# The first segment's attention by halves of its queries, each half through all heads, with the output projection to follow each half

## The chip, the cores and the metric

The kernel runs on one core of a Trainium2 chip. The metric is the device time of one launch in microseconds (us). A run has a *granted clock*: the mean share of TensorE's full clock that the chip allowed in that run.

Engine names are those of the profile: PE is TensorE (matmul), PEld its weight load, DVE is VectorE, ACT is ScalarE, POOL is GpSimd, SP is the queue that issues most transfers. L1205 is line 1205 of the kernel; the changed kernel has other line numbers for the same things.

## The reference, cut to what matters

T = 2048 tokens of D = 640, H = 32 heads of 20, four segments of L = 512, and a feed-forward width of 1728. Attention is causal inside a segment; a memory M carries over from segment to segment.

```python
def layer(x):
    x = x + attention(layernorm(x))     # wq, wk, wv, wo, memory
    x = x + relu(layernorm(x) @ w1) @ w2
    return x

def attention(xn):                       # for each head
    for s in range(4):
        p = softmax(q[s] @ k[s].T * scale + causal_mask)
        o = g * (phi(q[s]) @ M) / (phi(q[s]) @ z) + (1 - g) * (p @ v[s])
        outs.append(o)
        M = M + phi(k[s]).T @ v[s]; z = z + phi(k[s]).sum()
    return concat(outs) @ wo

out = layer(layer(x))                    # same weights in both layers
```

The first segment of the first layer has no memory yet. Nothing of its output projection, its second layer norm or its feed-forward can start before its attention is done, and at that point of the program there is little else to do but the projections of queries, keys and values.

## The kernel before

The kernel does not write its instruction order down. It describes each piece of work as a small generator, with the engines that may run it, a modelled duration, and what it needs and holds; a list scheduler inside the kernel builds the order on each engine. It makes 20 plans, and keeps the one that its own model says ends first. So any edit of a duration or a dependency may reorder the whole program. The parts that matter:

```python
HALVES = (0,)      # in segment 0 the scores go out four matmuls at a time, X and Y apart
...
# PSUM: X and Y (2 banks each) for scores, OD (1 bank) for p @ v, MISC (3 banks) for all else

def scores(m):                 # a pair of head groups (4 heads each), all 512 queries
    rounds = (((0, 0, 0),), ((0, 1, 0), (0, 3, 384)), ((0, 2, 0), (1, 2, 256)),
              ((1, 0, 0),), ((1, 1, 0), (1, 3, 384)))        # 5 rounds, each 512 columns wide
    ...
    def make(parts, ks):       # matmuls with K = 20: four heads in four row groups of the array
        ... e.matmul(ps[:, hh, o:o + N], kq(b, gg[x], 0)[32*hh:32*hh + DH, 128*j:128*j + 128],
                     kq(b, gg[x], 1)[32*hh:32*hh + DH, 128*j:L])
    def exp(u, k, bs, tk): ... # ACT: 1024 elements per partition into the tile PT
    def mask(x, j, ex): ...    # POOL: affine_select on the diagonal blocks of PT

def apply(n): ...              # p @ v: 128 x 32 matmuls in four column groups, into OD
def o_turn(a, s): ...          # waits for all heads, transposes o, then the output projection
```

One setup step is also touched by the change. `kqL` holds the query and key rows of the last heads, and it is cleared once, on POOL, before it is written:

```python
def consts():
    ...
    tl = yield pool(1600.0, lambda e: e.memset(kqL[:], 0.0))
    KQL[0].drop(tl)                                  # writers of kqL wait for it
    tm = yield pool(400.0, lambda e: e.memset(maskg[:], 0.0))
```

The softmax here doesn't subtract the row's maximum and nothing guards it: scores larger than these inputs give would overflow.

## Time and profile before

The time before was 592.19 us, the median of 3 runs (592.14 to 592.25). The page of the kernel before, its first two parts, begins like this; the second part gives the busy tenths in 40 equal slices:

```profile
span 591.0 us, 12433 instructions
...
PE 575.2 (97%) x5086; PEld 297.3 (50%) x5086; DVE 425.9 (72%) x1018; ACT 427.3 (72%) x520; POOL 215.5 (36%) x342
...
PE   8989999999999899999999999999999999999998
...
ACT  4869999989888888878787776897787787123140
...
PEclk9979999999999999999999999999999999999999
```

TensorE is called busy for 97% of the span. That busy time contains what happens inside pipelined matmuls, so I also computed a *useful share*: the columns streamed in a stretch, divided by 2.4 GHz and by the length of the stretch. 2.4 GHz is the clock that the prediction takes; the traces come close to it, as two whole matmuls of 512 columns start 0.216 us apart. Matmuls in row groups or column groups run four at a time (16 of `p @ v`, 5,120 columns in all, take 0.73 us) and are counted as a quarter. A matmul that runs over the edge of a stretch is counted in both, so the shares are about 0.01 too high. For 40 to 60 us the groups by shape of the kernel before begin with these (line, names, shapes, count, then busy time and mean):

```profile
L912 PE MATMUL ps<-wv_r,xnT 128*128 128x320 bf16 x21 | 5.2, 301 | 0.0
L878 PE MATMUL ps<-xnT,wk_p 128*128 128x512 bf16 x13 | 4.3, 385 | 0.0
L1011 PE MATMUL ps<-wb,hT 128*128 128x512 bf16 x10 | 3.3, 423 | 0.0
L878 PE MATMUL ps<-xnT,wq_p 128*128 128x512 bf16 x10 | 2.7, 380 | 0.0
...
```

These four rows stream 21 x 320 + 33 x 512 = 23,616 columns, or 9.8 us at 2.4 GHz. The scores add 2.1 us and the `p @ v` matmuls 2.1 us. So 14.0 of 20 us are streaming: a useful share of 0.70, where the page says 100% busy.

| Stretch (us) | 0–20 | 20–40 | 40–60 | 60–80 | 80–100 | 100–120 | 120–140 | 140–160 |
|---|---|---|---|---|---|---|---|---|
| useful share before | 0.52 | 0.58 | 0.70 | 0.75 | 0.87 | 0.78 | 0.83 | 0.90 |

One place stands out in the first 40 us. The timeline of the kernel before (start, duration, engine, line, operation, what it waited for) shows a POOL memset, two DVE items that last as long as it does, and TensorE waiting for one of them:

```profile
29.89 2.92 DVE L989 COPY hT<-ident 128x48 bf16<-128x48 bf16 x3
30.14 2.65 POOL L741 MEMSET kqL<- 128x3072 bf16 x1
30.23 2.76 DVE L826 TENSOR_SCALAR xn_tok<-x_sb,mv,rstd 128x640 bf16<-128x640 bf16 x1
33.04 0.45 PE L790 MATMUL ps<-ident,xn_tok 128*128 128x128 bf16 x5 [1.82 <-DVE xn_tok L826]
```

Just after it, the busy time by stretches (the number after POOL's is the granted clock) shows TensorE at half clock:

```profile
34.00:36.00 2.00, 2.00 (x22) 0.59 (x20) 1.28 (x3) 0.90 (x1) 0.96 (x2) 0.58 0.78 189
36.00:38.00 2.00, 2.00 (x16) 0.58 (x9) 1.61 (x9) 1.15 (x2) 0.08 (x1) 0.50 0.60 228
38.00:40.00 2.00, 2.00 (x6) 0.56 (x4) 0.18 (x2) 0.68 (x2) 1.22 (x2) 0.50 0.73 131
40.00:42.00 2.00, 2.00 (x14) 0.67 (x14) 0.41 (x1) 1.63 (x3) 0.00 (x0) 0.71 1.05 200
```

Finally, the chain of waits of the kernel before, between 46 and 68 us (start, duration, what), is almost only exponentials on ACT:

```profile
47.04 3.75 ACT PT L1219 x4
50.79 1.83 ACT PT L1216 x2
52.62 3.67 ACT PT L1219 x4
...
62.73 3.67 ACT PT L1219 x4
```

### The profile page before, as it was taken

To read this page: it belongs to the slowest core of one execution; us is meant where nothing else is said; L and a number is where in the kernel's file an instruction comes from. 1 tells how busy PE (TensorE), PEld (TensorE's weight loads), DVE (VectorE), ACT (ScalarE), POOL (GpSimd) and SP (SyncE) were. 2 spreads that over 40 slices of the span, in tenths; PEclk is the share of its full clock that TensorE was granted. 3 is DMA by queue.
4 is the path that set the end of the run, shared out by engine and by line. 5 is a ranking of instruction groups with operands and counts; after the bars stand their busy time and mean duration, and the time that the engine had idled before them with its cause. 6 is when DMAs were issued, how large, how long until landed. Compare 5 with 4: busy or idle time off the path is not lost.

```text
span 591.0 us, 12433 instructions
## 1 busy us (share of the span) xinstructions
PE 575.2 (97%) x5086; PEld 297.3 (50%) x5086; DVE 425.9 (72%) x1018; ACT 427.3 (72%) x520; POOL 215.5 (36%) x342
## 2 busy tenths in 40 slices
PE   8989999999999899999999999999999999999998
PEld 4423345434565354564444555455544654655655
DVE  6769769999979974899755985597827898734202
ACT  4869999989888888878787776897787787123140
POOL 4556644745343543344433440344322333002000
PEclk9979999999999999999999999999999999999999
DMA  6244593494743531256329314254408451331201
GB/s 211 91 110 102 101 166 66 57 216 95 106 84 70 110 64 37 41 109 118 63 32 150 52 26 88 43 94 89 68 2 105 101 92 31 84 69 23 68 0 45
DMA packets 126609, 48.44 MB, mean 82 GB/s; under 512 B 114056, under 2 KB 125256, under 8 KB 126552
## 3 DMA queue, kind: packets, MB, share of 16 engines
q1 hardware_dynamic: 124600, 40.10, 38.2%
q0 software_dynamic: 1520, 7.21, 4.0%
q8 instruction: 40, 0.66, 0.4%
q10 hardware_dynamic: 432, 0.34, 0.2%
q14 instruction: 17, 0.14, 0.1%
HBM read 13.77 MB, written 6.06 MB: 34 GB/s over the span
## 4 chain that ended last, share of the span: by engine, by line
PE 76%; DVE 13%; ACT 6%; DMA 3%; issue 1%; POOL 0%; SPq 0%
PE ps L1486 20%; PE ps L1466 16%; PE ps L878 13%; PE ps L1418 7%; PE ps L1205 7%; PE ps L1287 6%; PE ps L912 5%; ACT PT L1219 4%; DMA wb<-in_A_wk_dram 2%; DVE hT L1449 1%; ACT PT L1216 1%; DVE xn_tok L826 1%; DVE o_sb L1336 1%; PE ps L1155 1%; DMA oT<-o_sb 1%; DVE o_sb L1144 1%
## 5 line engine op out<-in xcount | busy, mean ns | idle before, releaser
L1219 ACT ACTIVATE PT<-ps 128x1024 bf16<-128x1024 f32 x256 | 248.3, 1031 | 49.9 <-PE ps L1205 49.1
L1195 POOL TENSOR_SCALAR_AFFINE_SELECT PT<-PT 128x512 bf16<-128x512 bf16 x256 | 172.2, 689 | 266.3 <-ACT PT L1219 220.1
L1466 PE MATMUL ps<-xnT,wb 128*128 128x512 bf16 x560 | 135.4, 380 | 3.0 <-DVE hT L1449 3.0
L1486 PE MATMUL ps<-wb,hT 128*128 128x320 bf16 x896 | 131.9, 299 | 0.6 <-DVE o_sb L1144 0.5
L1360 DVE TENSOR_TENSOR x_sb<-x_sb,ps 128x320 bf16<-128x320 bf16 x128 | 60.9, 479 | 69.8 <-PE ps L1486 53.4
L1486 PEld LDWEIGHTS ps<-wb,hT 128*128 128x128 bf16 x896 | 83.5, 98 | 39.6 <-issue 7.8
L1466 PEld LDWEIGHTS ps<-xnT,wb 128*128 128x128 bf16 x560 | 50.5, 98 | 63.5 <-issue 7.6
L1450 ACT ACTIVATE hT<-ps 128x512 bf16<-128x512 f32 x54 | 32.3, 598 | 56.8 <-PE ps L1466 56.5
L1216 ACT ACTIVATE PT<-ps 128x1024 bf16<-128x1024 f32 x64 | 62.2, 1028 | 10.9 <-PE ps L1205 10.7
L912 PE MATMUL ps<-wv_r,xnT 128*128 128x320 bf16 x320 | 60.3, 300 | 1.5 <-DVE va L900 0.6
L865 DVE CAST kq<-ps 128x512 bf16<-128x512 f32 x44 | 30.1, 686 | 36.4 <-PE ps L878 36.4
L878 PE MATMUL ps<-xnT,wk_p 128*128 128x512 bf16 x200 | 55.3, 381 | 0.0
L878 PE MATMUL ps<-xnT,wq_p 128*128 128x512 bf16 x200 | 54.8, 386 | 0.1
L1418 PE MATMUL ps<-wo_r,oT 128*128 128x320 bf16 x320 | 52.6, 300 | 1.2 <-DMA oT<-o_sb 0.9
L1449 DVE TENSOR_SCALAR hT<-ps 128x512 bf16<-128x512 f32 x58 | 39.4, 681 | 8.2 <-PE ps L1466 7.7
L912 PEld LDWEIGHTS ps<-wv_r,xnT 128*128 128x128 bf16 x320 | 29.6, 98 | 23.0 <-issue 3.9
L1287 PE MATMUL ps<-PT,va 128*32 128x128 bf16 (+3 forms) x896 | 40.7, 302 | 0.0
L826 DVE TENSOR_SCALAR xn_tok<-x_sb,mv,rstd 128x640 bf16<-128x640 bf16 x64 | 37.0, 590 | 4.8 <-DMA xnT<-xn_tok 3.6
L1418 PEld LDWEIGHTS ps<-wo_r,oT 128*128 128x128 bf16 x320 | 29.7, 98 | 18.6 <-issue 3.8
L1205 PE MATMUL ps<-kq 20*128 20x512 bf16 (+3 forms) x560 | 35.3, 301 | 0.1
L813 DVE BATCH_NORM_STATS2 stats<-x_sb 128x6 f32<-128x320 bf16 x64 | 29.7, 465 | 2.8 <-DMA x_sb<-in_A_x_dram 2.5
L1287 PEld LDWEIGHTS ps<-PT,va 128*32 128x32 bf16 x896 | 18.9, 96 | 23.7 <-issue 11.2
(100 smaller groups left out, 617.7 us busy)
## 6 DMA issues: line engine op xcount, KB each, us to landing
kq_scr<-kq SPq DMA_DIRECT2D x28, 120.0 KB
kqL<-kq_scr SPq DMA_DIRECT2D x28, 120.0 KB
out_dram<-x_sb SPq DMA_DIRECT2D x16, 160.0 KB, 1.8
wb<-in_B_w_dram POOLq DMA_DIRECT2D x5, 432.0 KB, 3.5
x_sb<-in_A_x_dram POOLq DMA_DIRECT2D x3, 640.0 KB, 5.5
wb<-in_B_w_dram POOLq DMA_DIRECT2D x2, 640.0 KB, 6.9
xnT<-xn_tok SPq DMA_TRANSPOSE x52, 2.7
wv_r<-in_A_wv_dram SPq DMA_DIRECT2D x1, 800.0 KB, 7.2
```

Of the source, the lines that this page charges most:

```text
L878: fn = lambda e, bank, k=k, w_p=w_p, c=c: e.matmul(bank, w_p[:, k, c * 128:(c + 1) * 128], xnT[:, k_, :, k, :], start=(k == 0), stop=(k == ...
L912: fn = lambda e, bank, k=k, i=i, hf=hf: e.matmul(bank[:, 0:320], xnT[:, k_, i, k, :], wv_r[:, k, hf * 320:(hf + 1) * 320], start=(k == 0), ...
L1195: tm = yield pool(590.0, lambda e: e.affine_select(out=reg, in_=reg, pattern=[[0, 4], [1, 128]], compare_op=ALU.is_ge, fill=0.0, base=0, c ...
L1205: fns.append((lambda e, x=x, j=j, hh=hh, N=N, o=o: e.matmul(ps[:, hh, o:o + N], kq(b, gg[x], 0)[32 * hh:32 * hh + DH, 128 * j:128 * j + 12 ...
L1216: fn = lambda e: e.activation(PT[:, :, 2 * k:2 * k + 2, 1024:1280], bs.ap.rearrange("p h (x t) -> p x h t", x=2), ACT.Exp, scale=SCALE)
L1219: fn = lambda e: e.activation(PT[:, items[0], 2 * k:2 * k + 2, c0:c0 + 512], bs.ap, ACT.Exp, scale=SCALE)
L1287: return [(lambda e, hh=hh, j=j: e.matmul(bank[32 * hh:32 * hh + 32, 128 * j:L], v_flat[b][:, (j * H + 8 * hh + g) * E1:(j * H + 8 * hh + ...
L1360: ta = yield dve(320, 1, lambda e: e.tensor_tensor(xa, xa, bk.ap[:, 0:320], ALU.add), [tk], early=HOT)
L1418: fn = lambda e, bank, k=k, hf=hf, o=ot.ap: e.matmul(bank[:, 0:320], o[:, k, :], wo_r[:, k, hf * 320:(hf + 1) * 320], start=(k == 0), stop ...
L1449: th = yield evac(512, 1, lambda e: e.tensor_scalar(hTv[:, dc, :], bk.ap, 0.0, None, ALU.max), lambda e: e.activation(hTv[:, dc, :], bk.ap ...
L1466: fn = lambda e, bank, k=k, dc=dc: e.matmul(bank, w1_r[:, k, dc * 128:(dc + 1) * 128], xnT[:, k_, :, k, :], start=(k == 0), stop=(k == FC ...
L1486: fn = lambda e, bank, dc=dc, i=i, hf=hf: e.matmul(bank[:, 0:320], hTv[:, dc, i * 128:(i + 1) * 128], w2_r[:, dc, hf * 320:(hf + 1) * 320] ...
```

## The change

The intent: take the queries of the first segment in two halves. The first half (256 queries) goes through all heads, then the second. The output projection of the first half can then start while the second half is in attention, and TensorE gets other work earlier. The rounds become 512 and 256 wide in the first half, and 512, 384, 512, 384 in the second. The output of each half is turned by TensorE transposes instead of DMA transposes. Two small things came along: the memset of `kqL` is dropped (it is not needed for the result), and the scheduler is told that weights land 1.7 us later. Core of the diff, cuts marked:

```diff
-        HALVES = (0,)
+        HALVES = tuple((m, v) for m in range(4) for v in range(2))
+        FFN_HALVES = ()
+        FIRST_ORDER = ((0, 0), (1, 0), (0, 1), (2, 0), (3, 0), (1, 1), (2, 1), (3, 1))
...
-            def ld(e, name, nbytes, fn, key, waits=(), issue=700.0, lat=2600.0):
+            def ld(e, name, nbytes, fn, key, waits=(), issue=700.0, lat=4300.0):
...
-            KQL[0].take()
...
-                tl = yield pool(1600.0, lambda e: e.memset(kqL[:], 0.0))
-                KQL[0].drop(tl)
...
-            def scores(m):
+            def layout(m, hv):      # hv: None for whole, 0 or 1 for a half
+                ...
+                if hv == 0:
+                    at = {(x, j): (m % 2, (256 * x, 512 + 128 * x)[j], 128 * j, 256 - 128 * j)
+                          for x in range(2) for j in range(2)}
+                    return at, (((0, 0), (1, 0)), ((0, 1), (1, 1)))
+                at = {(x, j): (x, 256 * j, max(256, 128 * j), 128 if j == 3 else 256) ...}
+                return at, (((0, 0), (0, 1)), ((0, 2), (0, 3)), ((1, 0), (1, 1)), ((1, 2), (1, 3)))
+            def scores(m, hv):
...
+            def turn_half(m, hv, g, od, tk):
+                ...
+                    return [(lambda e, i=i: e.transpose(
+                        bf(bank)[:, i * 128:(i + 1) * 128], rw.ap[:, 0, i * 128:(i + 1) * 128], ident[:]),
+                        i == NJ - 1) for i in range(NJ)]
+                ...
+                S.set("oh", hv, m, v=to)
...
                 for i in range(NJ):
+                    if a * NSEG + s == 0 and i % 2 == 0:      # o_turn: wait for this half only
+                        ow = []
+                        for m in range(G // 2):
+                            r = yield Need("oh", i // 2, m)
+                            ow += r
```

The feed-forward also learns to run by halves (`FFN_HALVES`), but that list is left empty.

## The prediction

> **What bounds the kernel now.** The page gives TensorE 97% busy, but that counts waits inside pipelined matmuls. I divided the columns streamed in each stretch (groups by shape) by the 2.4 GHz of the Trainium skill, "TensorE: Matmul & The Clock Gate" (score and apply matmuls four at a time). The useful work is then about 58% of the time in 20–40 us, 70% in 40–60, 75% in 60–80, 78–87% in 80–140, and 0.86–0.93 afterwards. So TensorE bounds the kernel from about 80 us on, and the recoverable loss is early: against 0.89, some 15 us between 20 and 130 us. There the exponentials on ACT set the pace (chain of waits: 47–67 us is almost only ACT PT; ACT busy 0.9–1.0 of 40–120), because nothing of output projection or feed-forward can start until the first segment's attention is finished: exponentials of segment one end at 66 us, first output projection matmul at 94.5 us, first W1 matmul at 115.7 us.
>
> A second loss, beside it: the timeline shows the POOL memset of kqL taking 2.65 us at 30.1–32.8, and in just that time small DVE copies (L989) and one normalisation (L826) take 2.9 and 2.8 us instead of about 0.1 and 0.45. "SBUF — State Buffer", section "Who interferes with whom", states that a GpSimd instruction and a 2-port DVE instruction exclude each other; the trace agrees. TensorE waits 1.82 us there for xn_tok, and the granted clock is 0.5 from about 34.3 to 41 us (windows of 1 us): about 3 us more.
>
> **What the change does.** It removes that memset and builds the selectors of the relay at the very start, where DVE is idle. It adds 8 exponentials (48 in place of 40 in the first segment, same elements; fixed part of one about 0.1 us: 1 us on ACT), 32 transposes of 128x128 on TensorE (0.09 us each: 3 us, in slack), and takes away 4 DMA transposes with their latency. The narrower exponentials (about 0.5 and 0.7 us instead of 0.94) leave less time to refill the other PSUM pair: an estimated 2 us of ACT idle. The first exponential comes about 0.8 us later (both heads' groups needed).
>
> What it moves: by instruction order, when the first segment's exponentials are all issued, TensorE has done 11 us more useful work than before (49.6 against 38.7), 12 us more after the second segment's; still 9 at half of the attention, 5 at three quarters. ACT has 8 us more done at the first of these points.
>
> **On the critical path.** ACT must do about 102 us of work to the end of the second segment's exponentials (97 before). I expect that point at about 121 us (before 120.5) with work done that before had at about 131 us. Later DVE (0.95–1.0 busy in 90–160 us) and ACT, lagging, give back a part. Net gain 5 to 10 us: predicted 584.5 us, range 577.5 to 591. Faster by over 2% 0.20, within 2% 0.77, slower 0.03.
>
> **What would show it.** Useful TensorE share in 20–80 us up from 0.68 to about 0.75–0.8; no 2.7 us DVE copies at 30 us and no half clock in the 30–40 us stretch (TensorE waits under 1 us); first output projection near 75 us or earlier; first W1 matmul at 105–112 us; segment-one exponentials ending at 70–76 us; ACT busy +1 to +2 us in total; stretches after 160 us shifted, not changed.
>
> **What would make it wrong.** A new TensorE gap in the first 40 us with another half-clock spell (slower: gain gone). ACT idling at each narrow round, more than 5 us in total. Orders made for modelled durations, in which in-order waits on DVE give the lead back at 100–160 us. Or the gain lies mostly in the memset: then the halves alone give nothing.

## More of the kernel before

Scores, `p @ v` and all other matmuls use the array in three different groupings: by row groups, by column groups, and whole. The scheduler knows that changing costs something; it reckons 100 ns for each change (`MODE_NS = 100.0`).

## The result, and the profile after

The changed kernel took 591.65 us, the median of 4 runs (590.17 to 592.00), beside 592.22 us for the kernel before on the same chip (4 runs, 592.14 to 593.39). The ratio is 0.9981 with a 95% interval of 0.996 to 1.0002: the same time. A ratio here and below is the mean time of one kernel's fast runs over that of the other's of the same rounds, so it is not quite the ratio of the medians that I quote. The prediction, 584.5 us with a range of 577.5 to 591.0, was missed: the measured median lies above the range.

The page of the changed kernel, its first lines and the granted clock:

```profile
span 590.3 us, 12794 instructions
...
PE 576.7 (98%) x5257; PEld 302.2 (51%) x5257; DVE 424.4 (72%) x1027; ACT 429.7 (73%) x531; POOL 210.2 (36%) x341
...
PEclk9999999999998999999999999999999999999999
```

The stall at 30 us is smaller, and the half clock behind it is gone. But at 187 us a new wait of TensorE appears. The timeline of the changed kernel:

```profile
30.52 1.50 DVE L750 CAST maskg<-gt 20x160 bf16<-20x160 f32 x1
...
33.08 0.45 PE L789 MATMUL ps<-ident,xn_tok 128*128 128x128 bf16 x5 [1.24 <-DVE xn_tok L825]
...
187.15 0.59 PE L1543 MATMUL ps<-xnT,wb 128*128 128x512 bf16 x2 [1.38 <-DMA xnT<-xn_tok]
```

Its busy time by stretches has full clock after the first wait and half clock after the second:

```profile
34.00:36.00 2.00, 2.00 (x16) 1.30 (x14) 1.89 (x8) 1.92 (x5) 0.00 (x0) 1.00 0.41 146
...
186.00:188.00 2.00, 0.78 (x10) 0.24 (x10) 2.00 (x10) 1.76 (x2) 1.52 (x3) 1.00 0.51 132
188.00:190.00 2.00, 2.00 (x26) 0.74 (x19) 2.00 (x5) 1.75 (x2) 1.08 (x2) 0.53 0.66 128
190.00:192.00 2.00, 2.00 (x6) 0.59 (x4) 1.38 (x4) 0.19 (x1) 1.22 (x2) 0.62 0.59 82
```

| | before | after |
|---|---|---|
| last exponential of segment one ends (us) | 66.4 | 76.0 |
| last exponential of segment two ends | 120.5 | 129.9 |
| first output projection matmul | 94.5 | 63.0 |
| first W1 matmul | 113.6 | 107.4 |
| useful share 20–40 us | 0.58 | 0.78 |
| useful share 40–60, 60–80 | 0.70, 0.75 | 0.70, 0.74 |
| useful work done by 40 / 80 / 180 / 260 us | 21.8 / 50.4 / 133.9 / 202.4 | 25.9 / 54.0 / 139.2 / 204.8 |

The lead of 4.1 us of useful work is made before 40 us, where the memset was. It does not grow in 40 to 80 us, where the halves are at work, and it falls to 2.3 us between 180 and 260 us, the stretch that begins with the half clock. Of what is left, about 1.7 us is the 32 added transposes of 128 columns (32 x 128 / 2.4 GHz), which are not useful in the end.

The chain of waits of the changed kernel in the same part of the program is no longer ACT's. It runs through many short pieces of TensorE:

```profile
57.07 0.33 PE ps L1347 x4
57.40 0.32 PE ps L1221 x4
57.72 0.54 PE ps L877 x2
58.48 0.27 PE ps L1221 x4
58.75 0.54 PE ps L877 x2
59.69 0.50 PE ps L1314 x16
60.19 0.32 PE ps L877
```

### The profile page after: what moved, and what is told of

Same layout as the page of the kernel before. It is cut to its first block, busy times and chain, and to the rows that moved or that the text cites. A ratio compares the mean times of both kernels' runs of the same rounds, so it can differ in the third digit from the quotient of the medians.

```text
span 590.3 us, 12794 instructions
## 1 busy us (share of the span) xinstructions
PE 576.7 (98%) x5257; PEld 302.2 (51%) x5257; DVE 424.4 (72%) x1027; ACT 429.7 (73%) x531; POOL 210.2 (36%) x341
## 4 chain that ended last, share of the span: by engine, by line
PE 73%; DVE 18%; ACT 6%; issue 1%; POOL 1%; DVEq 0%
PE ps L1543 17%; PE ps L1565 17%; PE ps L877 13%; PE ps L1221 7%; PE ps L911 6%; PE ps L1314 5%; PE ps L1489 5%; ACT PT L1239 4%; DVE x_sb L1426 2%; DVE hT L1517 2%; ACT etmp L1057 1%; DVE stats L812 1%; DVE stats L813 1%; DVE xn_tok L825 1%; DVE phq L1124 1%
## 5 line engine op out<-in xcount | busy, mean ns | idle before, releaser
L1239 ACT ACTIVATE PT<-ps 128x1024 bf16<-128x1024 f32 (+1 forms) x272 | 256.3, 1000 | 45.0 <-PE ps L1221 43.7
L1209 POOL TENSOR_SCALAR_AFFINE_SELECT PT<-PT 128x512 bf16<-128x512 bf16 x256 | 168.8, 677 | 269.6 <-ACT PT L1239 229.4
L1543 PE MATMUL ps<-xnT,wb 128*128 128x512 bf16 x560 | 137.9, 382 | 2.0 <-DMA xnT<-xn_tok 1.4
L1518 ACT ACTIVATE hT<-ps 128x512 bf16<-128x512 f32 x53 | 31.7, 599 | 52.8 <-PE ps L1543 52.6
L1236 ACT ACTIVATE PT<-ps 128x1024 bf16<-128x1024 f32 x56 | 54.3, 1025 | 14.9 <-PE ps L1221 14.7
L1489 PE MATMUL ps<-wo_r,oT 128*128 128x320 bf16 x320 | 54.0, 300 | 0.9 <-DVE x_sb L1426 0.7
L877 PE MATMUL ps<-xnT,wk_p 128*128 128x512 bf16 x200 | 53.8, 381 | 0.0
L864 DVE CAST kq<-ps 128x512 bf16<-128x512 f32 x46 | 31.5, 684 | 22.6 <-PE ps L877 22.0
L825 DVE TENSOR_SCALAR xn_tok<-x_sb,mv,rstd 128x640 bf16<-128x640 bf16 x64 | 30.6, 492 | 5.8 <-POOL rstd L821 5.1
```

Of the source, the lines that this page charges most:

```text
L877: fn = lambda e, bank, k=k, w_p=w_p, c=c: e.matmul(bank, w_p[:, k, c * 128:(c + 1) * 128], xnT[:, k_, :, k, :], start=(k == 0), stop=(k == ...
L1209: tm = yield pool(590.0, lambda e: e.affine_select(out=reg, in_=reg, pattern=[[0, 4], [1, 128]], compare_op=ALU.is_ge, fill=0.0, base=0, c ...
L1236: fn = lambda e: e.activation(PT[:, :, 2 * k:2 * k + 2, c0:c0 + n], bs.ap.rearrange("p h (x t) -> p x h t", x=2), ACT.Exp, scale=SCALE)
L1239: fn = lambda e: e.activation(PT[:, slots[0], 2 * k:2 * k + 2, c0:c0 + n], bs.ap[:, :, 0:n], ACT.Exp, scale=SCALE)
L1489: fn = lambda e, bank, k=k, hf=hf, o=ot.ap: e.matmul(bank[:, 0:320], o[:, k, :], wo_r[:, k, hf * 320:(hf + 1) * 320], start=(k == 0), stop ...
L1543: fn = lambda e, bank, k=k, dc=dc, i0=i0, i1=i1, n=n: e.matmul(bank[:, 0:n], w1_r[:, k, dc * 128:(dc + 1) * 128], xnT[:, k_, i0:i1, k, :], ...
```

## The experiments

Eighteen kernels ran, each with its own runs of the kernel before on the same chip. All gave correct results. "Planned anew" means that the edit let the scheduler make another order; "order kept" means that it did not.

The kernel before ran 43 times, and its runs fall apart by the granted clock: 23 runs at 0.994 had a median of 592.29 us, 11 at 0.997 had 590.87, and 9 at 1.000 had 589.43. In the traces the half clock in mid-run comes in spells of 3.41 us (changed kernel, a_H, a_mem, a_ffnh) or 6.83 us (kernel before, b_whole), which cost about 1.7 and 3.4 us; one spell of 3.41 us more or less is also about what separates the three groups, 1.4 us each. No trace was taken of a run of the kernel before at 1.000, but its clock leaves no room for the half clock that the traced run shows at 34 us. So I compare kernels both as they are and at equal clock.

### The parts of the change

**b_small: the kernel before, with the memset cut to a sliver, order kept.** The scheduler still models 1600 ns, so it makes the same order. Is the stall at 30 us all that the change gains, and how much is it?

```diff
-                tl = yield pool(1600.0, lambda e: e.memset(kqL[:], 0.0))
+                tl = yield pool(1600.0, lambda e: e.memset(kqL[:, 0, 0, 0:32], 0.0))
```

> The kernel before, every instruction in the same order on every engine; only the POOL memset of kqL writes 32 columns instead of 3072. Theory A (the memset, through the DVE stall, the PE wait and the half clock after it, is the loss that the changed kernel has recovered by 40 us): no 2.9 us DVE copies at 30 us, PE wait at 31-33 us gone, no half clock at 34-41 us, useful TensorE share of 20-40 us up from 0.58 to 0.70 or more, and total 587.5 to 589.5 us if the lead lasts. Theory B (the halves make the lead): the stall goes but total stays within 1 us of 592.

Measured: 587.45 us (6 runs, 587.18 to 587.80), the kernel before 591.1 (11 runs), ratio 0.994 (0.992 to 0.9961), and a clock of 1.000 in all six. The timeline of b_small shows the same three items without the stall:

```profile
28.99 0.39 DVE L989 COPY hT<-ident 128x48 bf16<-128x48 bf16 x3
29.23 0.12 POOL L741 MEMSET kqL<- 128x32 bf16 x1
29.31 1.07 DVE L826 TENSOR_SCALAR xn_tok<-x_sb,mv,rstd 128x640 bf16<-128x640 bf16 x1
```

One line, without any halving, gains more than the whole change. By 40 us b_small has 25.3 us of useful work done (before: 21.8, after: 25.9), and its first W1 matmul is at 107.9 us (after: 107.4). So nearly the whole lead of the change is the memset, 3.5 of 4.1 us, and W1 came hardly earlier for the halves. At equal clock the stall is worth 589.43 - 587.45 = 2.0 us; the rest of the 3.6 us is the half clock that it brings in most runs.

**b_M, b_ML and n_p12: all but the halves, planned anew.** b_M removes the memset and its hold on `kqL`. b_ML also takes the later weight landing, so it is the change without halves. n_p12 is b_ML with the scheduler's second best plan.

```diff
-            KQL[0].take()
...
-                tl = yield pool(1600.0, lambda e: e.memset(kqL[:], 0.0))
-                KQL[0].drop(tl)
# b_ML and n_p12 also:
-            def ld(e, name, nbytes, fn, key, waits=(), issue=700.0, lat=2600.0):
+            def ld(e, name, nbytes, fn, key, waits=(), issue=700.0, lat=4300.0):
# n_p12 also:
-            if best is None or end < best[0]:
+            if n == 12:
```

> The kernel before without the memset of kqL (its part of the change), planned anew. Theory A: 587 to 590 us. Theory B: 592. Theory C (any new plan moves the later order by a few us at random): may be anywhere from 588 to 595 though its first 40 us are as good as with the small memset.

> All of the change but the halves: no memset of kqL and the assumed landing time of the weights 4300 instead of 2600 ns. Theory A: within 2 us of the changed kernel (591.6), or faster. Theory B (the halves bring a gain and the rest nothing): slower than the changed kernel by 3 us or more.

> All of the change but the halves, second best plan in place of the best. Theory C: 587 to 595 us, overlapping with the orders that have the halves. If the halves are worth several us: all orders without them slower than all with them.

Measured: b_M 592.01 us (591.69 to 593.05, ratio 1.0023), b_ML 590.58 (590.01 to 592.32, ratio 0.9996), n_p12 590.61 (588.68 to 592.95, ratio 0.9984). With the memset dropped and the order made anew, the gain of b_small is gone: b_M, at clock 1.000 in all six runs, is slower than the kernel before at that clock (589.43), and so is b_ML. b_M has nearly the same lead as b_small by 80 us (54.6 us of useful work, b_small 55.0), and loses it between 100 and 120 us, where its useful share is 0.65 against 0.75. So kernels that do the same work, without the stall and without halves, differ by 4.6 us (b_small to b_M; 5.2 with b_p7 below) through the order alone. This spread limits what can be said of anything smaller that was planned anew.

**a_H: the halves alone.** The memset with its hold and the earlier weight landing are put back into the changed kernel, which is planned anew.

```diff
-            def ld(e, name, nbytes, fn, key, waits=(), issue=700.0, lat=4300.0):
+            def ld(e, name, nbytes, fn, key, waits=(), issue=700.0, lat=2600.0):
...
+            KQL[0].take()
...
+                tl = yield pool(1600.0, lambda e: e.memset(kqL[:], 0.0))
+                KQL[0].drop(tl)
```

> The halves alone: the changed kernel with the memset of kqL and the old assumed landing time put back. Theory A: the stall of DVE by the memset comes back somewhere before 40 us; 593 to 597 us. Theory B: as fast as the changed kernel, 590 to 592 us.

Measured: 592.98 us (592.57 to 595.53), ratio 1.0044 (1.0019 to 1.0068). The halves alone gain nothing; in this order they lose 2 us, and against the kernel before at clock 1.000 about 3.5. The time fell just short of the 593 to 597 us of theory A, but its trace (a run at 0.997) shows that theory's mechanism: in a quite different order, beside the same memset, a DVE cast takes as long as the memset, TensorE then waits 1.53 us for DVE, and the half clock follows from 30.6 to 34.0 us.

```profile
26.76 2.65 POOL L744 MEMSET kqL<- 128x3072 bf16 x1
26.79 2.66 DVE L868 CAST wb<-ps 128x512 bf16<-128x512 f32 x1
```

**a_mem: the changed kernel with POOL kept busy before the mask's memset, order kept.** Two memsets of other tiles (1.79 and 0.65 us as they ran) are put in, to bring the stall back.

```diff
-                tm = yield pool(400.0, lambda e: e.memset(maskg[:], 0.0))
+                tm = yield Op([("pool", 400.0, 60.0, lambda: [
+                    (lambda e: e.memset(otok[:], 0.0), False), (lambda e: e.memset(BD[:], 0.0), False),
+                    (lambda e: e.memset(maskg[:], 0.0), True)])], [], ())
```

> The changed kernel, every other instruction in the same order; ahead of the POOL memset of maskg stand two more memsets (otok and BD, together about 2.3 us on POOL). Theory A (a long memset at this time stalls DVE and through it PE, also with the halves): DVE copies of over 1.5 us beside it, PE wait near 30 us of 2 us or more, probably a half-clock spell; total 594 to 596 us. Theory B (the halves have made the kernel insensitive to it): within 1 us of 591.6.

Measured: 593.26 us (592.10 to 595.54), ratio 1.0028, clock 0.997 in 4 of 6 runs. The waits of TensorE in a_mem, and two stretches of it:

```profile
PE ps L791 <- DVE xn_tok L827: 2.4, 2, 1.9
```

```profile
34.00:36.00 2.00, 1.54 (x12) 1.06 (x13) 2.00 (x7) 1.05 (x2) 0.00 (x0) 0.89 0.81 313
36.00:38.00 2.00, 2.00 (x8) 0.90 (x7) 1.85 (x8) 1.18 (x3) 0.00 (x0) 0.50 0.00 0
```

A longer wait of TensorE near 33 us brings the half clock into the changed kernel too. The time lies between what the two theories gave (594 to 596, and within 1 us of 591.6). The dose was not clean, though: DVE waited 1.80 us for POOL's mask directly, so this run does not show a stall by shared ports.

**a_nospell: the changed kernel, with TensorE given something to do in the wait at 186 us, order kept.** A matmul of the memory read is repeated 36 times into the same place. Is that wait, through the half clock after it, what holds the changed kernel above 590?

```diff
-                                start=(g == 0), stop=True, skip_group_check=True), g == 3) for g in range(4)]
+                                start=(g == 0), stop=True, skip_group_check=True), g == 3)
+                                for g in [0] * (36 if (a, s, h, i) == (0, 2, 1, 3) else 0) + list(range(4))]
```

> The changed kernel with 36 repeats of one small memory-read matmul put into the PE wait at 186 us (same result). Theory D (the wait is what brings the half clock at 188-191 us, seen in three of four runs): the granted clock of all runs is 1.000 and the time is 590.2 as in the one undisturbed run of the changed kernel. If it is not the wait, 591.6 and clock 0.997.

Measured: 589.99 us (589.87 to 590.43), ratio 0.9974, clock 1.000 in all six. One of its stretches at the same place, with full clock:

```profile
188.00:190.00 2.00, 2.00 (x27) 0.78 (x19) 2.00 (x5) 1.70 (x2) 0.82 (x2) 1.00 0.47 85
```

Useless work in the wait made the kernel 1.7 us faster and its runs steadier. So the half clock costs that much. With the half clock gone, the lead over the kernel before is still 5.4 us of useful work by 260 us (the added transposes counted). But 589.99 is 2.5 us above b_small, which has neither the halves nor this order.

**a_p5: the changed kernel in its second best plan.** How much is the order's luck with halves?

```diff
-            if best is None or end < best[0]:
+            if n == 5:
```

> The changed kernel with the second best of its own plans in place of the best: same work, another order. Theory C (orders differ by some us at random): 587 to 596 us. If the order counted for little: 591 to 592.5.

Measured: 591.17 us (589.83 to 592.29), ratio 0.9991. No other order was seen in which the halves do clearly better.

### Who sets the pace in the first segment

The prediction held that ACT does. The test is to add a known amount of work to one engine in one stretch, order kept, and see what share of it the whole kernel gets longer by. An engine that sets the pace returns nearly all of it. TensorE's work is the first matmul of an accumulation, done again with `start` set before the real one, which does not change the result. ACT's and DVE's is small instructions into a tile of their own. The first four start from a_nospell, so that no half clock disturbs them. The edits are shown condensed.

```diff
# s_pe1 (TensorE, 40-76 us; s_pe2 the same with another range of instructions and one repeat each, 80-130 us)
+            if it[0] == "op" and 290 <= n < 738 and hasattr(it[1], "again"):
+                new += [("op", it[1].again, None, 0)] * 2
# s_act1 (ACT, 40-76 us; s_act1b later: after every instruction, 46 of them)
+            if it[0] == "op" and 51 <= n < 97 and n % 2 == 0:
+                new.append(("op", lambda e, c=c: e.activation(padA[:, c], gt[:, 1, 0:8], ACT.Copy), None, 0))
# s_dve2 (DVE, 80-132 us)
+            if it[0] == "op" and 161 <= n < 272 and n % 7 == 0:
+                new.append(("op", lambda e, c=c: e.bn_stats(padD[:, c], maskg[:]...[:, 0:320]), None, 0))
```

> Sensitivity, on the changed kernel with the PE wait at 186 us filled (589.99 us, clock 1.000; its order is kept): 23 small ACT instructions (about 0.2 us each, 3.5 to 5 us in all) are added between 40 and 76 us, where the first segment's exponentials run. Theory E (ACT sets the pace of the first segment): the time grows by at least 60% of the ACT time added, to 592.5 to 595 us. If not, below 591.5.

> Same base; 38 repeats of first matmuls of accumulations (about 6 to 7 us of TensorE) are added between 40 and 76 us. Theory E: TensorE has room there (useful share 0.70), the time grows by less than 40% of that, to below 592.5 us. If TensorE's queue is what paces this stretch in spite of the 0.70: 595 us or more.

> Same base; 16 DVE instructions of 0.4 us (6.4 us in all) are added between 80 and 130 us, where the prediction expected the lead to grow and it did not. Theory F (in this stretch DVE, busy 0.9 and more, holds TensorE back through evictions and normalisations): time grows by over 50% of it, to 593 us or more. Otherwise within 1.5 us of 590.

> Same base; 33 repeats of first matmuls (about 5.5 us of TensorE) are added between 80 and 130 us. If TensorE itself is the limit there (useful share 0.81 to 0.9 being all that such a mixture reaches): 594 to 596 us. Theory F: TensorE has some room, grows by under 50%, below 593 us.

After these results the rival theory was that TensorE itself sets the pace, in b_small too, where there are no halves. Two runs put the same kind of work into b_small (40 to 62 us), and s_act1b repeated the ACT dose at twice the size, since s_act1's came out smaller than meant.

```diff
# bs_pe1 (b_small)
+            if it[0] == "op" and 288 <= n < 493 and hasattr(it[1], "again"):
+                new += [("op", it[1].again, None, 0)] * 3
# bs_act1 (b_small)
+            if it[0] == "op" and 46 <= n < 73:
+                for _ in range(2):
+                    new.append(("op", lambda e, c=c: e.activation(padA[:, c], gt[:, 1, 0:4], ACT.Copy), None, 0))
```

> Sensitivity without the halves: the kernel before with the small memset (587.45 us, order kept), 33 repeats of first matmuls (5.5 to 6.5 us of TensorE) added between 40 and 62 us, in the first segment's attention. Theory G (TensorE's own queue paced this stretch already before the change, short matmuls and switches filling what I took for room): grows by over 60%, to 591 us or more. Theory E' (it was ACT that paced it, and only the halves have moved the limit to TensorE): grows by under 40%, below 590 us.

> Same base, 54 small ACT instructions (0.10 us of ACT each beside its neighbours, as measured in the run before: 5.4 us) added between 40 and 62 us. Theory G: grows by under 50%, below 590.2 us. Theory E': over 60%, 590.7 us or more.

> The changed kernel (wait filled, 589.99 us) with 46 small ACT instructions between 40 and 76 us, twice the dose of before (4.6 us): if the share of before holds (0.8 us for 2.3 us), 591.6 us; if ACT had just been brought to its limit there, 592.5 us or more.

| Run | Engine and stretch | Added (us) | Time (us, median of 4) | Longer by | Share |
|---|---|---|---|---|---|
| s_act1 | ACT, 40–76, with halves | 2.3 | 590.80 | 0.8 | 0.35 |
| s_act1b | ACT, 40–76, with halves | 4.6 | 592.00 | 2.0 | 0.44 |
| s_pe1 | TensorE, 40–76, with halves | 6.6 | 595.82 | 5.8 | 0.88 |
| s_dve2 | DVE, 80–132, with halves | 6.4 | 592.65 | 2.7 | 0.42 |
| s_pe2 | TensorE, 80–130, with halves | 6.5 | 595.33 | 5.3 | 0.82 |
| bs_pe1 | TensorE, 40–62, no halves | 6.2 | 593.04 | 5.6 | 0.90 |
| bs_act1 | ACT, 40–62, no halves | 5.4 | 591.50 | 4.05 | 0.75 |

"Longer by" is against a_nospell (589.99) or b_small (587.45), which ran on other chips; the kernel before had medians of 591.0 to 591.9 in all these. The amounts are worked out from the traces: the matmuls added are 0.216 us each for 512 columns and 0.136 for 320, and a small ACT instruction took up 0.10 us of ACT in its stream.

A share is uncertain by some 0.1 to 0.2: the four runs of bs_pe1 alone lie between 591.82 and 593.83 us.

TensorE returns 82 to 90% of what it is given, between 40 and 130 us with the halves and between 40 and 62 us in b_small. It has no room there, with or without halves. In a_nospell and then in s_pe1, the stretches show ACT yielding (the fourth busy time in a row, after PE, PEld and DVE, is ACT's):

```profile
40.00:50.00 10.00, 9.92 (x117) 4.08 (x117) 7.62 (x18) 9.50 (x13) 5.52 (x9) 1.00 0.56 137
60.00:70.00 10.00, 9.96 (x134) 4.89 (x133) 5.75 (x13) 9.34 (x13) 4.96 (x9) 1.00 0.19 59
```

```profile
40.00:50.00 10.00, 10.00 (x111) 4.64 (x112) 6.61 (x16) 8.68 (x11) 4.09 (x7) 1.00 0.47 123
60.00:70.00 10.00, 10.00 (x131) 5.13 (x129) 3.39 (x8) 8.76 (x11) 3.36 (x6) 1.00 0.17 52
```

ACT was not a mere follower in b_small: it returned 0.75, and bs_act1 came out at the figure set for the theory that ACT paces this stretch (590.7 us or more). By this test ACT and TensorE can't be told apart there; both hold it. The reading offered is that the two engines hand the two PSUM pairs of the scores to and fro, so that either one delays the other. With the halves ACT's share is smaller (0.44), but the dose was also thinner (4.6 us over 36 us, against 5.4 over 22), so a weaker grip of ACT is likely and not shown. s_dve2 and s_act1b lie between the figures set for their theories: DVE in 80 to 132 us returns 0.42, so it is neither the limit nor free.

The chain of waits would not have told this. In b_small it is, from 46 to 62 us, still almost only ACT, in the very stretch where TensorE returned 0.9.

### What TensorE spends its time on

So what is the missing 30% of TensorE's useful share? I added up, from the timeline, the time from one group of matmuls to the start of the next, less the recorded waits. In b_small between 17 and 62 us, TensorE is *occupied* for 44.0 of 45 us in this sense, and waits 0.7 us. A stretch of its timeline:

```profile
48.15 0.39 PE L1205 MATMUL ps<-kqL 20*128 20x384 bf16 x4
48.47 0.60 PE L1011 MATMUL ps<-wb,hT 128*128 128x512 bf16 x2
48.91 0.30 PE L912 MATMUL ps<-wv_r,xnT 128*128 128x320 bf16 x1
49.15 0.39 PE L1205 MATMUL ps<-kqL 20*128 20x384 bf16 x4
49.47 0.73 PE L1287 MATMUL ps<-PT,wb 128*32 128x512 bf16 x16
```

The four score matmuls at 48.15 us stream 384 and 128 columns for two heads at once, 512 columns in all, 0.213 us at 2.4 GHz. The next group starts 0.32 us later. The array changes from whole to row groups and back for every such run. "TensorEngine Tiling (Array Packing)" in the Trainium skill, section "Tiling Modes", says under its key properties that changing the tiling mode "drains the TensorE", and gives no figure. The traces agree, and let it be estimated, if all the time beyond streaming is put down to changes of grouping:

| | b_small 17–62 us | after 18–77 us | b_whole (below) 17–62 us |
|---|---|---|---|
| occupied (us) | 44.0 | 56.9 | 43.7 |
| streaming at 2.4 GHz | 32.2 | 43.0 | 38.1 |
| changes of grouping | 74 | 92 | 39 |
| difference per change | 0.16 | 0.15 | 0.14 |

About 0.15 us for each change, in three kernels with very different numbers of them. That is an estimate, but it says where the 30% is: not room, but the price of short runs. Taken matmul by matmul, the traces bear out that the time lies at the changes: 10.7 of the 12.4 us beyond streaming in b_small, and 12.6 of 14.0 in the changed kernel. Going to row groups costs about 0.10 us, coming back 0.17 (medians), and from one whole matmul to the next it is 3 ns.

The halves raise that price. The first segment's attention takes 11.46 us of scores and 5.28 of `p @ v` in b_small; in a_nospell it takes 10.75, 6.79, and 2.03 of added transposes. That is about 2.8 us more on an engine that has no room, and it is close to the 2.5 us between b_small and a_nospell.

**b_whole: b_small with the scores of the first segment in runs of eight matmuls, planned anew.** This halves the number of changes there. If they are the price, TensorE must get ahead in the first segment.

```diff
-        HALVES = (0,)
+        HALVES = ()
-                tl = yield pool(1600.0, lambda e: e.memset(kqL[:], 0.0))
+                tl = yield pool(1600.0, lambda e: e.memset(kqL[:, 0, 0, 0:32], 0.0))
```

> The kernel before with the small memset and with its own switch for splitting the first segment's score rounds into two PSUM pairs set off (X and Y filled together: half as many, twice as long score runs on TensorE), planned anew. Theory G (switches on TensorE cost time there): score runs of the first segment 8 matmuls each instead of 4, TensorE time for them down by about 3 us, total 586 to 589 us; but a new plan can hide it (587 to 592 us were seen for equal work). If ACT waiting for the longer runs counts for more: 590 us or more.

Measured: 591.24 us (589.25 to 594.01), ratio 1.0. TensorE does get ahead: 44.1 us of useful work by 60 us, against 38.8 in b_small, a useful share of 0.90 in 40 to 60. Then the share falls to 0.53 and 0.48 in 80 to 120 us. The groups of b_whole in that stretch show why: 92 filler matmuls (the scheduler puts them in where TensorE has nothing to do), and a wait for a layer norm:

```profile
L722 PE MATMUL ps<-ident 128*128 128x128 bf16 x92 | 6.2, 219 | 0.0
...
L790 PE MATMUL ps<-ident,xn_tok 128*128 128x128 bf16 x20 | 2.1, 243 | 3.3 <-DVE xn_tok L826 3.3
```

The work that is ready early was used up early, and the half clock came again (0.83 on average in 100 to 120 us). So the first segment's pace is one limit, and behind it stands another: the serial path through normalisation to the next segment.

### Does the earlier output projection bring the feed-forward forward?

**a_ffnh: the changed kernel with the first feed-forward by halves too, planned anew.** If W1 were held up only by the second half's tiles, it would now start much earlier.

```diff
-        FFN_HALVES = ()
+        FFN_HALVES = (0,)
```

> The changed kernel with its own switch set so that the first segment's feed-forward also runs by halves, planned anew. Theory H (the halves gain nothing because the first W1 matmul still waits for all four tiles: 107.4 us against 107.9 us with the small memset alone): first W1 matmul at 95 us or earlier and 588 us or less. Theory G (TensorE time is what counts, and this adds 70 narrower matmuls and weight loads): first W1 earlier, but the time 590 to 594 us.

Measured: 590.84 us (590.54 to 592.34), ratio 1.0009. The first W1 matmul is still at 107.28 us, although the first two tiles that it needs were turned at 68 and 77 us and its weights had landed by 70 us. The theory's premise fell: W1 does not wait for missing tiles. The timeline shows TensorE full of projections of the later segments, with W1 behind them. The reading is that bringing one kind of ready work forward on a full engine only pushes another kind back.

### The best version seen

**b_p7: b_small in its second best plan.**

```diff
-                tl = yield pool(1600.0, lambda e: e.memset(kqL[:], 0.0))
+                tl = yield pool(1600.0, lambda e: e.memset(kqL[:, 0, 0, 0:32], 0.0))
...
-            if best is None or end < best[0]:
+            if n == 7:
```

> The kernel before with the small memset and the second best of its plans: same work, another order. Theory C: anywhere from 587 to 593 us; it shows how far 587.45 was the order's luck.

Measured: 586.84 us (586.39 to 587.72), the kernel before 591.64 (7 runs), ratio 0.9919 (0.9893 to 0.9946). It beats both kernels, without the halves.

## Why the prediction was wrong

The step that failed is the one that sized the gain: "the recoverable loss is early: against 0.89, some 15 us between 20 and 130 us", with "There the exponentials on ACT set the pace". What I took for room was occupied. TensorE returned 0.82 to 0.90 of the work added between 40 and 130 us, and ACT 0.35 to 0.44 with the halves in place. That ACT held the first segment before the change was not false in itself (0.75 in b_small); false was that TensorE had room beside it. Dividing streamed columns by 2.4 GHz corrects the busy time of pipelined matmuls, but it hides about 0.15 us (an estimate) for each change of the array's grouping, and there are 74 of those between 17 and 62 us of b_small. The page's 97% was nearer the truth here than my 70%.

Point by point:

- *The memset stalls DVE, TensorE waits, and the half clock follows.* Right. b_small shows 3.6 us for it. The stall fits what "SBUF — State Buffer" in the Trainium skill, section "Who interferes with whom", states of GpSimd and 2-port DVE instructions: the one that issues first holds the shared ports, and the other is blocked until it ends (2.65 us for the memset, 2.92 and 2.76 us for the DVE items, 0.39 and 1.07 us in b_small). That ports are the cause was not tested by itself.
- *No half clock at 30 to 40 us, TensorE waits under 1 us.* The clock was right, the wait was 1.24 us. A DVE cast still took 1.50 us at 30.5 us.
- *Segment-one exponentials end at 70 to 76 us; first output projection by 75; first W1 at 105 to 112.* Right in place: 76.0, 63.0 and 107.4. But b_small, without halves, has its W1 at 107.9. (The prediction's 115.7 us for the kernel before is the second group of W1 matmuls; the first starts at 113.6.) A mark can be met for another reason than the one that it was meant to show.
- *"I expect that point at about 121 us", the end of segment two's exponentials.* Wrong: 129.9 us. That TensorE held ACT back fits the doses, which showed TensorE without room.
- *Useful share in 20 to 80 us "up from 0.68 to about 0.75–0.8".* The mean of the three stretches rose from 0.68 to 0.74, just short. All of the rise was in 20 to 40 us, from the memset. In 40 to 80 us it stayed at 0.70 and 0.74.
- *"3 us, in slack" for the transposes.* Wrong in the word slack: the transposes took 2.0 us, but there was no slack on TensorE. With the scores and `p @ v` of the halves, about 2.8 us more of it were needed.
- *ACT busy +1 to +2 us, a fixed 0.1 us for each added exponential.* Measured +2.4 in total. The exponentials are as predicted: where the next one follows at once, it starts 0.70 us after one of 768 elements, 0.50 after one of 512 and 0.91 after one of 1024, and all of them together cover 1.1 us more of ACT than before. The other 1.3 us are evictions and other pieces that the new order gave to ACT.
- *"A new TensorE gap in the first 40 us with another half-clock spell".* The kind of event was right, the place was not: it came at 186 us, and a_nospell shows 1.7 us for it.
- *"Or the gain lies mostly in the memset: then the halves alone give nothing."* This came true: a_H is 2 us slower than the kernel before, and removing the stall alone (b_small) gains 3.6.

The sum, in medians: removing the stall, with the order kept, takes the usual run from 592.2 to 587.45 (b_small). The changed kernel without its wait at 186 us, which has the halves and an order made for them, is 2.5 slower than that (589.99, a_nospell). The wait at 186 us adds 1.7 in the runs where the half clock comes (591.65). At equal full clock, the change is no gain at all: 589.43 before, 590.17 in the one run of the changed kernel at 1.000, 589.99 in a_nospell.

Left open: how much of the 2.5 us is the halves and how much is the luck of the order. Kernels without halves and without the stall came out between 586.84 and 592.01 us, those with halves between 589.99 and 591.65. No run isolates the halves with all else kept, and the nearest comparison speaks against a cost: b_ML and n_p12, all of the change but the halves, took 590.58 and 590.61, a little more than a_nospell.

The kept traces settle one part of it. The first segment's scores, `p @ v` and added transposes occupy TensorE for 19.6 to 20.0 us in every kernel with halves (the changed kernel, a_nospell, a_p5, a_ffnh, a_H), and for 16.4 to 16.9 in five orders without them (b_small, b_p7, b_M, b_ML, n_p12; b_whole has other score runs and is set aside). So the 3 us or so belong to the halves and not to one order. By 80 us the useful work, added transposes left out, is 52.6 to 53.1 us with the halves and 54.6 to 56.6 without (a_H, which has the stall, set aside). By 180 us the two groups overlap (135.4 to 138.1, and 135.0 to 138.6). What the halves cost in the first segment is thus shown; how much of it reaches the end depends on the later order, and is not shown.

Nor does the scheduler's own model, which picks the order, tell a few tenths: the plan that it ranked second (b_p7, 586.84) was no slower on the chip than the one that it ranked first (b_small, 587.45). It did give a hint before any run, though. Run again without the chip, it ends the kernel before at 579.4 us and a_H, which adds the halves alone, at 581.7.

## What to carry to other kernels

A low share of streamed columns is not yet room: before counting on it, add up from the timeline how long the engine is occupied from start to start, or add a known dose of work and see what share comes back. Splitting small matmuls further, to start the next stage earlier, is paid on TensorE with every change of the array's grouping, and on a full engine the stage that starts earlier may only displace other ready work, as W1 in a_ffnh. When a change carries small side edits, run each alone and with the order kept: here one shortened memset gained more than the whole change, and the same memset dropped with a new order (b_M) gained nothing.

## What the Trainium skill lacked or had wrong

- "TensorE: Matmul & The Clock Gate", section "What's actually happening": the table gives half clock after at least one idle window of about 3.4 us. Here waits of 1.82 us (kernel before), 1.53 us (a_H) and 1.38 us (changed kernel) were followed by it in the traces, while waits of 1.24 us (changed kernel) and 1.54 us (s_pe2, at 317 us) were not, so these runs give no threshold. By their clocks, 34 of 43 runs of the kernel before and 3 of 4 of the changed kernel had a half clock somewhere. The page's free-running window would fit that the same wait brings it in some runs only, but the table does not say that a single, much shorter wait can be enough.
- "TensorEngine Tiling (Array Packing)", section "Tiling Modes": it states that a change of mode drains TensorE, but gives no cost. An estimate from these traces is 0.14 to 0.16 us for each change, which was about 12 of the 45 us from 17 to 62 us in b_small.
- "Perfetto Trace Analysis", section "Identifying the Most-Contended Engine": it says that matmul busy time does not tell how close a kernel is to its roofline, and has headroom on TensorE judged by MFU and weight-load busy time. Here a useful share of 0.70, a figure of the kind of MFU, with weight loads busy for 36% (7.22 of 20 us in the kernel before) suggested headroom, and there was none: added TensorE time came back at 0.9. A measure between the two, occupied from start to start less the waits, is missing.
